# A listed order of 2,500 steps found anew: attention followed by a gated feed-forward block on one core

## The chip, the core and the metric

The kernel runs on one core of a Trainium2 chip. A core has a matrix engine (TensorE, "PE" in the profile; its weight loads are shown as "PEld"), VectorE ("DVE"), ScalarE ("ACT"), GpSimd ("POOL") and SyncE ("SP"), which here only issues DMA transfers. Every engine takes its own instructions strictly in the order in which the program lists them, and waits at an instruction until the semaphores that it names have come. The metric is the device time of one execution in microseconds (us). Before the change the median of three runs is 685.67 us (685.07 to 685.78).

## The reference

Two blocks follow each other, all in float32. The first is an attention between 512 tokens and 32 states in each of 8 batches and 8 heads, in both directions. The second takes the 8 x 544 = 4,352 rows that come out of it (544 rows a batch, 512 wide) through a feed-forward layer of width 2,048 with an unusual gate.

```python
def _attn_ref(x, state):            # x (8, 8, 512, 64), state (8, 8, 32, 64)
    scores = scale * np.matmul(x, state.transpose(0, 1, 3, 2))
    a = softmax(scores)             # over the states
    xread = np.matmul(a, state)
    scores2 = scale * np.matmul(state, x.transpose(0, 1, 3, 2))
    a2 = softmax(scores2)           # over the tokens
    sread = np.matmul(a2, x)
    return np.concatenate([xread, sread], axis=2)

def _moe_ref(x, w_in, w_out):       # x (4352, 512)
    h = x @ w_in                    # 512 -> 2048
    sp = np.maximum(h, 0.0) + np.log1p(np.exp(-np.abs(h)))
    g = h * erf(sp)
    return g @ w_out                # 2048 -> 512
```

## The kernel before, in words

**Work and stages.** The token rows of a batch are one unit, A1 to A7 and B0 to B7: the hidden layer is cut in two halves of 1,024, and the A units do the first half for all batches, the B units the second. (Batch 0's first half is done apart, in the head, by the steps h0 to h7 and o00 to o36; the state rows have units of their own, SA and SB.) Each A unit of batch b comes with the attention of batch b; the attention's weights y are kept in DRAM and come back for the B units. The state matrix is multiplied with w_in once a batch (the steps ending in m, called "mixed"), so that xread is never written out: h is y times that product. The large products are cut in the way of Strassen and Winograd: seven products of half blocks instead of eight, with sums and differences before and after. In the first product of a unit these are the steps f01 to f17, in the second one (done twice over, quarter blocks) ap10 to bp71. So TensorE does fewer products, and VectorE many additions: 582 of its 763 instructions are tensor_tensor.

**Steps and the list.** Every piece of work is a named step, registered with `step(name, f)` and issued in the order of one string, `ORDER`, with 2,532 names. The string was written by a planner that is not part of the kernel. The last lines of the kernel read it and tie each engine's instructions to that order. A name `~k*n` is no step: it issues n filler products on bank k, whose results nobody reads.

```python
    for name in ORDER.split() or do:
        if name[0] == "~":
            k, n = name[1:].split("*")
            issue(name, lambda: warm(bank[int(k)][:, 0:P], int(n)))
        else:
            issue(name, do.pop(name) if ORDER.split() else do[name])
    in_order(begun)
```

The list interleaves all engines, so it tells two things: the order on each engine, which binds, and where the planner thought a step on one engine would start beside those on the others, which does not. In the trace of the kernel before, the steps of VectorE and ScalarE start within 3.6 us of the TensorE step listed next, mostly 0.4 to 1.1 us ahead of it.

**Names that the change and the prediction touch** (lines are those of the profile):

- Loads. lx0 to lx3 (L341): batch 0's x in four pieces of 256 KB, lx0 and lx2 on ScalarE's queue, lx1 and lx3 on SyncE's. lst0 (L346): batch 0's state, 64 KB; ls1 (L369): batch 1's; lst1 to lst8 (L365): the rest, on GpSimd's queue. i0l0 to i3l1 and o0l0 to o3l1 (L394): halves of w_in and w_out, 512 KB each. a1xq0 to a1xq7 (L354): batch 1's x, in small pieces, two transfers a step, all on SyncE's queue.
- Conversion of each half weight: a0 and a1 on ScalarE (L379, L381), v0 on VectorE (L383), v1 on VectorE or, for i2, i3 and o0 to o3, on GpSimd (L385).
- Batch 0's attention. x00 to x31 transpose the pieces (L444), s0 the state (L450), the steps ending in c copy the results out of PSUM. t0 and t1 (L456) are the token scores, 16 products of 64 columns each as the trace counts them, q0 and q1 (L463) the state scores. Each half k of the tokens runs through max, less (subtract), exp (ScalarE), sum, inv, norm, ta (transposes, L469) and tac (copy to y).
- First unit. n00, n01, n02, n10, n12 (L961): w_in mixed with the state; h0L to h7R (L972): h products, which need both y (tac) and the mixed pieces; h0s to h7s softplus (L693), h0e and the like erf (L988), each behind a table load of ScalarE when the function changes. big0 to wn1, tw0, tw1, rd0 (L539), rn0, rt0 (L549): batch 0's state attention. a1tx0 to a1tx3 (L250) transpose batch 1's x; a1s (L564) are batch 1's scores.
- Attention of batch b, after the scores: a2sb0 and a2nm0 and the like (L587, L596) subtract the maximum and multiply by the inverse sum; from batch 2 on they run on GpSimd. These twelve and the six conversions are GpSimd's 18 tensor instructions.
- VectorE's additions with two operands in SBUF: t01 to t64 (L243; sums of w_out's blocks, `twice`, L934), y01 and the like, A1a2, A1b3, A2b4+ and the like (`inner_sums`), A1g0 and the like (the gate, L244).
- Stores. res holds seven half blocks of results. A1D0 and the like (L735) add a half block to the output in DRAM, on GpSimd's queue; A1d0 and the like write it first, on SyncE's. The copy that reuses the place in res (A1ac11, A1au2) waits until the store has landed.
- The end: B7p71 is TensorE's last step; B7C120, B7C121, B7v20 to B7v31 are additions, B7d10 to B7d31 the last stores.

Of the kernel before, what the change touches and what calls it, by code (L numbers as in the profile page):

```python
# [52 lines left out]
A1bp71 a3ty0 A1bp51 A1bu3 y31 A3f01 a3kz A3m01 A1b4 A2f1s12 A1D0 A1bp20 A3M1 A3f0c t54 A2f1s22
A1bp21 y32 A1bp40 A3M2 A1b4+ A1bp41 A3M3 A2e0 A3f06 y34 A1bc22 A3f02 A3M4 y33 A1bp30 A3f0c11 A2g0
a3z2 A3f0u2 a3z1 A3f05 A2e1 a3z0 a3z3 A3f07 A1d3 a4tx2 A3f11 A3f0u3 A1bp31 A1bc21 A3f0c22 A3f04
A1bc11 a3iy A1bc12 A2ap10 A3f0c21 A2g1 A1d1 A3f1c A3f03 yl3 A3f16 rd3 A2q A3f1u2 A3f17 A3f0c12
rn31 rn30 A2A1 rt3 A2ap50 A3f1u3 rc3 A1D1 A2A3 A3f14 A2ap11 A3f0s11 A2A2 A2ap51 A2ac A2a2 A3f12
A2A4 A3f15 a4s A1U2 A2a3 A1D4 A2ap60 a4c0 A3f0s21 a5xq6 A2b2 A2ap61 a4c1 A3f1c22 A2ap20 A2au2
# [6 lines left out]
A4f0u2 A2bp30 A2D0 A2bc11 A4M4 A4f0c11 A4f07 a5tx2 A2bp31 A4f0u3 A4f11 A2bc12 a4z1 a4iy a4z2 A4f04
A4f0c22 a4z3 A3g1 a4z0 A4f03 A4f0c21 A2d3 A2d1 A3ap10 A4f1c yl4 A4f16 A4f0c12 A4f12 A4f0s12 A2U2
A4f1u2 A3q A4f15 A4f0s11 A4f0s22 A4f17 A2U3 A4f0s21 A3A1 rd4 A4f1u3 A2D1 a5tx0 A4f14 rn40 rn41
A2D2 A3ap11 A3A3 rt4 A3ap50 rc4 A3a2 A4f1c11 A3ac a5s A4f1c22 A3ap60 A3a3 a5c0 a6xq1 a5c1 A3ap61
A3A2 A4f1c21 a6xq7 A2D3 A3ap20 A3au2 a6xq3 a5tu0 A4f13 a6xq2 A3A4 A3ap21 A3ap70 A3ac11 a5mx0
A4f1s11 A3ap71 A4f1s12 a6xq0 A4f1c12 a5sb0 A3ap51 A4f1s22 a5my0 A3au3 a6xq5 A3bp10 A4f1s21 A3ac22  # L70
A3bp11 A3ap40 A3a4 A2D4 a5ex0 A3ap41 A3b2 a5x2 A3ap30 A3ac21 a6xq4 a5sm0 A3bc A3ap31 a5ey0 a5iz
A3bp60 A3b4+ a5ey1 A3ac12 a5nm0 A3bp61 a6tx0 A3bp20 A3bp21 A4e0 a5x1 A3bp50 A3b3 a5x3 A3d2 A5m
a5ta0 A3d3 A3bu2 A3b4 A3bp51 a5ty0 A5m00 A3bp70 a5ty1 A5m10 A5m11 y51 A3bp71 a5kz A5f01 A5M1 a6xq6
A3bu3 A5m01 y52 A3bp40 A5M2 A5f0c A4e1 A3bc22 A3bp41 a5iy A5f06 y53 A5M3 A5f02 A5M4 A5f0u2 A5f05
A4g0 A5f0c11 A5f07 a5z0 A3bp30 a5z3 A5f0u3 A3d0 y54 A3bc11 A5f0c22 A3bp31 a5z2 a5z1 A5f04 A3bc12
a5x0 A4g1 A5f11 A5f0c21 A4ap10 A5f1c A3bc21 A5f03 A3d1 A4q A5f16 yl5 A3D0 A5f0s12 A5f0c12 A5f12
# [6 lines left out]
A6m01 A4bp50 A6M1 a6ty0 A6f01 A4b3 a6kz A5e0 A4bp51 a7xq0 A6f05 y62 A6M2 A4D0 a7xq4 A4bp70 a6iy
A6M3 A6f0c A4bp71 A6M4 A4bc11 a7xq5 A6f06 A4b4+ A4bu3 y63 A6f02 a7xq7 A4b4 A6f0u2 y64 A4bp40 A5g0
A6f0c11 A6f07 a6z0 a6x2 A6f11 a6z2 A6f0u3 a6x3 A4bc22 A5e1 A4bp41 a6z3 A6f0c22 A6f04 a6z1 a7tx0
yk5 A4bp30 A4bc21 A5g1 A6f0c21 A6f03 A6f1c A4bp31 A6f16 A6f0c12 A6f12 A6f0s22 A4bc12 A6f1u2 A5ap10
A5q A4d1 yl6 A6f17 a7tx2 rd6 A6f1u3 A6f1c11 A5A1 A6f15 rn61 a7x2 rn60 A4U2 rt6 A5ap50 rc6 A6f1c22
# [1 line left out]
A4U3 A6f0s11 a7tu0 A6f1s22 A5ap61 A4D4 A5ap51 A5a3 A5au2 i5+l A4D3 A6f1s12 A5ap21 a7x3 A6f1s11
a7mx0 A5ap70 A6f0s12 A5ac11 A6f1c12 a7sb0 A5ap71 a7my0 A6f1s21 A5bp10 A5au3 A5ac22 A5bp11 A5ap40  # L90
A5a4 A4D2 a7x0 a7ex0 A5ap41 A5b2 a7ey0 A5ap30 a7ey1 A5b4+ A5ap31 a7sm0 A5ac21 A7m A5bc a7iz A5ac12
a7nm0 A5d0 A6e0 a7x1 A5bp60 A5d2 A5bp20 a7ta0 A7m01 A5bp50 A7m00 A5bp21 A7m10 a7ty0 A5d3 A5bp51
A7m11 y71 A5bp61 A5b3 A7f01 A5bu2 y73 A5bp70 A7M1 yk7 y72 A5bp71 A7M2 A7f05 A5D0 A5bu3 A7M3 A7f0c
A5bp40 A5b4 A6e1 a7ty1 A7f06 A5bc22 a7kz A5bp41 A7M4 A7f0u2 A7f02 y74 A6g0 A7f07 A7f0c11 A5bp30
# [1085 lines left out]
```

## Time and profile before

| what | value |
|---|---|
| median of three runs | 685.67 us (685.07 to 685.78) |
| the profiled execution's own time | 685.86 us |
| its span, first to last instruction | 684.0 us |
| TensorE products | 5,586, busy 675.3 us |
| VectorE, ScalarE, GpSimd busy | 583.7, 488.4, 126.2 us |
| granted TensorE clock, mean | 0.999 |
| first product, end of the last product | 0.78 us, 679.07 us |
| ScalarE table loads | 63 (1.28 us each) |
| filler products in the list | 8 at the start, then 2 + 3 + 1 + 3 + 1 |

The span leaves out what the device does before the first and after the last instruction of the program; the time of a run holds it. A group's row on the page has the line, the engine, the operation, what it writes and reads, its busy time and the mean of one, and the idle time before it. A timeline row has the start, the length and the same names; "x5" merges five instructions that follow each other. In a row of the windows stand, for each engine, its busy time and in brackets the number of instructions that started in it, then the granted TensorE clock, the share of the DMA engines and the GB/s. A name ending in q means that an engine's sequencer only issued something.

### The profile page before, as it was taken

What the parts mean: (1) busy time and instruction counts of PE and PEld (TensorE: products, weight loads), DVE (VectorE), ACT (ScalarE), POOL (GpSimd) and SP (SyncE); (2) the same over time, 40 slices, a digit from 0 to 9 for tenths busy, and PEclk for the clock granted to TensorE, in tenths of its full rate; (3) what the DMA queues carried; (4) which work ended last, traced back from release to release, by engine and by line L of the source; (5) the groups of instructions that cost most, each with busy time, mean ns of one, the idle gap of its engine ahead of it and who ended that gap; (6) DMA issues with size and microseconds to landing.
All of it is one profiled execution on the core that took longest, in us unless ns stands there. A gap on an engine that the chain in (4) does not pass through costs nothing.

```text
span 684.0 us, 13840 instructions
## 1 busy us (share of the span) xinstructions
PE 675.3 (99%) x5586; PEld 591.3 (86%) x5586; DVE 583.7 (85%) x763; ACT 488.4 (71%) x759; POOL 126.2 (18%) x103
## 2 busy tenths in 40 slices
...
GB/s 301 201 253 125 194 143 172 180 106 186 173 162 132 178 210 176 185 116 140 199 218 222 108 103 84 2 67 20 47 101 62 55 36 82 20 66 16 78 55 124
DMA packets 145839, 87.15 MB, mean 127 GB/s; under 512 B 92784, under 2 KB 138096, under 8 KB 145776
## 3 DMA queue, kind: packets, MB, share of 16 engines
...
q10 hardware_dynamic: 544, 0.52, 0.2%
...
## 4 chain that ended last, share of the span: by engine, by line
PE 87%; DVE 4%; ACT 3%; SPq 3%; DMA 2%; issue 1%; DVEq 0%
PE b L827 44%; PE b L704 24%; PE b L757 5%; PE b L1034 4%; PE b L655 3%; PE b L994 3%; SPq L354 2%; PE b L972 1%; DVE big L250 1%; PE b L539 1%; PE b L564 1%; SPq L359 1%; DMA big<-kept_z 1%; PE b L431 1%; PE b L456 1%
## 5 line engine op out<-in xcount | busy, mean ns | idle before, releaser
L735 POOL DMA_DIRECT2D out_dram<-res x67 | 80.4, 1385 | 433.5 <-DVE res L242 128.0
L827 PE MATMUL b<-big,ring 128*128 128x128 f32 x1196 | 152.7, 276 | 0.0
L827 PEld LDWEIGHTS b<-big,ring 128*128 128x128 f32 x1196 | 145.5, 192 | 6.6 <-issue 2.5
L250 ACT COPY ring<-b 128x512 f32<-128x512 f32 (+1 forms) x136 | 78.4, 584 | 76.2 <-PE b L704 52.6
L704 PE MATMUL b<-y,m 128*128 128x256 f32 x480 | 122.0, 381 | 0.2 <-DVE ring L242 0.2
L250 ACT COPY res<-b 128x512 f32<-128x512 f32 (+2 forms) x125 | 64.2, 522 | 55.8 <-PE b L827 44.0
L704 PEld LDWEIGHTS b<-y,m 128*128 128x128 f32 x480 | 86.7, 191 | 13.0 <-DVE ring L242 1.3
L704 PE MATMUL b<-sy,m 128*128 128x256 f32 x360 | 91.5, 381 | 0.4 <-DVE m L243 0.4
L244 DVE TENSOR_TENSOR ring<-ring 128x2048 f32<-128x2048 f32 (+1 forms) x36 | 77.8, 2168 | 6.9 <-ACT ring L712 5.6
L693 ACT ACTIVATE ring<-ring 128x512 f32<-128x512 f32 x128 | 77.4, 632 | 3.0 <-DVE ring L242 2.5
L827 PE MATMUL b<-ta,ring 128*128 128x128 f32 x548 | 72.3, 276 | 0.0
L704 PEld LDWEIGHTS b<-sy,m 128*128 128x128 f32 x360 | 64.8, 191 | 8.3 <-issue 1.1
L827 PEld LDWEIGHTS b<-ta,ring 128*128 128x128 f32 x548 | 68.5, 192 | 3.8 <-issue 1.7
L827 PEld LDWEIGHTS b<-big,ta 128*128 128x128 f32 x572 | 68.2, 192 | 4.1 <-ACT b L250 1.7
L827 PE MATMUL b<-big,ta 128*128 128x128 f32 x572 | 71.3, 276 | 0.0
L243 DVE TENSOR_TENSOR ring<-ring 128x1024 f32<-128x1024 f32 (+3 forms) x66 | 69.9, 1068 | 0.2
L242 DVE TENSOR_TENSOR ring<-ring,b 128x512 f32<-128x512 f32 (+1 forms) x72 | 47.3, 660 | 23.9 <-ACT ring L250 12.2
L242 DVE TENSOR_TENSOR res<-res,b 128x512 f32<-128x512 f32 (+2 forms) x60 | 36.2, 603 | 33.5 <-PE b L827 18.8
L712 ACT ACTIVATE ring<-ring 128x2048 f32<-128x2048 f32 x30 | 57.3, 1912 | 0.2
L250 ACT COPY b<-b 128x512 f32<-128x512 f32 (+2 forms) x63 | 34.7, 551 | 21.2 <-PE b L827 13.9
L242 DVE TENSOR_TENSOR res<-res 128x512 f32<-128x512 f32 (+1 forms) x56 | 42.1, 753 | 1.1
L242 DVE TENSOR_TENSOR ring<-ring 128x1024 f32<-128x1024 f32 (+1 forms) x35 | 40.0, 1144 | 0.6 <-ACT ring L250 0.3
(150 smaller groups left out, 999.1 us busy)
## 6 DMA issues: line engine op xcount, KB each, us to landing
...
big<-in_x_dram SPq DMA_DIRECT2D x112, 64.0 KB, 2.7
...
```

Of the source, the lines that this page charges most:

```text
L242: add = lambda o, a, b: tt(o, a, b, op=ALU.add)
L243: sub = lambda o, a, b: tt(o, a, b, op=ALU.subtract)
L244: mul = lambda o, a, b: tt(o, a, b, op=ALU.mult)
L250: do[name] = lambda: f(*args)
L655: pe.matmul(out=to[j][e][q, :], lhsT=by, rhs=w_in[r, 4 * j:4 * j + 4, i, :], start=True, stop=True)
L693: act.activation(out=o, in_=i, func=ACTF.Softplus)
L704: pe.matmul(out=to[:, i], lhsT=xs[n - 1][:, q:q + P], rhs=ys[n - 1], start=(start and i == 0), stop=(i == 1), skip_group_check=True)
L712: step(u + "e%d" % o, lambda s=s: act.activation(out=s, in_=s, func=ACTF.Erf))
L735: nc.gpsimd.dma_start(out=to, in_=of, accum_op=ALU.add)
L757: pe.matmul(out=to[:, E2 * h:E2 * h + E2], lhsT=a[:, k // 2, k % 2], rhs=rhs[n][:, k], start=(start and h == 0 and k == 0), stop=(k == 3), ...
L827: pe.matmul(out=out_[:, P * j:P * j + P], lhsT=lhs[:, i], rhs=rhs[:, i], start=(start and j == 0 and i == 0), stop=(i == 1), skip_group_ch ...
L1034: pe.matmul(out=to[:, P * i:P * i + P], lhsT=xs[n - 1][:, i, k], rhs=ys[n - 1][:, k], start=(start and i == 0 and k == 0), stop=(k == 1), ...
```

## The change

Only the string `ORDER` differs. The set of steps is the same, and every step does what it did; the new list has 2,530 names, since there are three filler entries instead of five (2 + 1 + 3 products after the first 8). [...]

In the built program the order differs on every engine from the first steps on; on average a step stands about ten places from where it stood. TensorE has 2,812 product instructions instead of 2,816 (the fillers), ScalarE 60 table loads instead of 63, and the instructions that only wait for a further semaphore change in number: 114 instead of 128 on TensorE, 176 instead of 189 on VectorE, 196 instead of 184 on ScalarE, 124 instead of 109 on SyncE, 98 instead of 97 on GpSimd.

The diff, cut to the head, to the places named above and below, and to the end:

```diff
--- before.py
+++ after.py
@@ -21,161 +21,161 @@
 
 
 ORDER = """
-warm own lx2 lst0 lx3 lx0 lx1 i0l0 i0l1 i1l1 i1l0 x20 s0 x20c s0c0 i2l1 x30 x21 x30c x10 x31 x10c
-x00 s0c1 x31c x11 i2l0 x00c x11c t0 s0c i0a0 i3l1 x21c x01 i0v0 i0a1 max0 x01c i0v1 i0+a0 ~7*2 t1
-i3l0 less0 i0+v0 n00 exp0 max1 q0 n00c0 ls1 i0+a1 sum0 q1 less1 i1a0 inv0 i0+v1 exp1 norm0 o0l1
-~7*3 n01 i1a1 sum1 o0l0 ~7*1 ta0 a1xq0 inv1 q1c n01c1 norm1 n01c0 ta0c n00c1 i1v0 ~7*3 ta1 a1xq3
-i2a0 i1v1 h1L i2a1 h0L i2v0 q0c n02 ta1c i2v1 h0R big0 n02c0 i3a0 big1 ub h1R n02c1 i3a1 ubc a1xq2
-big h3L i3v0 wt0 a1xq5 h0c i3v1 n10 wt1 h1c h3R a1xq7 n10c1 n10c0 h2L o0a1 h3c a1xq6 wz o0a0 ~7*1
-n12 a1xq4 wn1 h5L n12c1 n12c0 a1xq1 y01 tw1 y02 wn0 o1l1 h2R o1l0 h1s y04 o0v0 h0s yl0 tw0 tw1c
-a1tx3 o3l0 o0v1 h3s h5R o3l1 h2c h2s o2l0 a1tx2 h6L tw0c a1tx1 rd0 h5c a1tx0 h0e h7L a1x2 rn0 t01
-a1x3 h2e rt0 h0g h6R rc0 h7R o1a0 h2g a1s o1a1 o1v0 h4L h7c a1c1 o1v1 h6c a1c0 h4R a1tu1 a2xq0 o00
...
-a2xq5 A1f11 a1iy o2v0 A1f0u3 a1x1 A1f0c22 A1f04 o2v1 h4c A1f03 h4s u1c a1z0 A1f0c21 u0c a1z2 o10
-A1f0c12 a1z3 A1f1c a1z1 t11 yl1 T1 A1f16 h6e a2tx2 o3v1 A1f15 h4e o12 a2tx0 A1f1u2 h6g A1f17
...
-A1f1c12 A1f1s11 a3xq1 a2mx0 A1f1s21 a2x2 o14 a2my0 a2sb0 t2k a3xq2 A1e0 t0k o26 a3xq4 t21 A1e1
-A1g0 a3xq6 o06 a2x0 a3xq5 A2m A1g1 yk0 a2ex0 yk1 a2x1 o16 A2m11 a2sm0 a2x3 o0c t3k A2m10 a2ey1 o30
...
-a3ey1 A1ap30 A1ac21 t53 a3iz A1bc A1ap31 t43 A1b3 a3ey0 A1bp60 A2f1c12 a3nm0 A1bp61 A1ac12 A3m
...
-A2ac21 a4sm0 A2ap30 a5xq5 a4ey0 A2ap31 a4ey1 a4iz A2b3 a5xq2 A2bc A4m a4nm0 A2ac12 a5xq4 A3f1s12
-A2bp60 A4m00 A4m01 A2bp50 A2b4+ A4m11 a4ta0 a5xq7 A4m10 A2bp61 A3f1s21 A2bp20 a5xq0 a4ty0 A2bu2
...
-a6ey0 A4ap41 a6sm0 a6ey1 A4ap30 A4ac21 a6iz A4b2 A4ap31 a6nm0 A6m A4ac12 A5f1s21 A4d2 A4bc A5f1s11
...
-A6f0s21 A6f14 A5A2 A4D1 A5ap11 A5a2 yk6 A6f13 A5ac A5A3 A6f1c21 a7s A5A4 A5ap60 a7c0 a7c1 A5ap20
...
-SBpc21 SBd2 B1f16 w13 w14 SBd1 B0ap50 B1f0s22 w23 B1f0c12 B1f1u2 B1f12 w3k SBd3 w42 w4k w03 B0ap11
...
-B7p31 B7pu2 B7w2 B7p70 B7C120 B7w4 B7d10 B7D1 B7C121 B7p71 B7d11 B7v30 B7v20 B7d30 B7v31 B7d20
-B7v21 B7d31 B7d21
+warm lx1 own lx2 lst0 lx3 lx0 i0l0 i0l1 i1l0 i1l1 i2l0 x10 s0 x10c x30 s0c1 s0c0 x11 x30c x20 x00
+x20c x31 i2l1 x00c x21 x11c t0 x31c i0a0 s0c i3l0 i0a1 i0v0 x21c i0v1 i0+a0 x01 i3l1 max0 x01c
+i0+v0 i0+a1 ~7*2 t1 less0 ls1 i0+v1 exp0 o0l0 sum0 i1a0 n00 max1 q0 i1a1 inv0 q1 less1 norm0 exp1
+n01 a1xq7 i1v0 n01c0 ~7*1 ta0 q1c sum1 o0l1 a1xq6 n01c1 ta0c inv1 n00c1 i2a0 norm1 ~7*3 h1L i1v1
+ta1 n00c0 i2a1 i2v0 h0L ta1c q0c i2v1 a1xq3 i3a0 n02 big0 ub h1R big1 i3a1 h0R n02c1 a1xq5 ubc
+n02c0 big i3v0 wt0 n10 a1xq1 h1c h3L i3v1 n10c0 wt1 h0c a1xq4 h2L o0a0 a1tx3 h2R o1l0 a1xq2 n10c1
+o0a1 h3R wz wn0 a1xq0 n12 wn1 h5L o3l1 n12c1 y01 o1l1 h3s tw1 y02 o2l1 n12c0 a1tx2 h0s tw0 h2s
+o0v0 tw1c h5R h2c o0v1 tw0c h3c h1s h6L a1tx1 rd0 a1tx0 h5c h0e h7L a1x1 rn0 y04 h2e o2l0 h0g rt0
+h6R a1x3 rc0 o3l0 o1a0 h7R h2g a1x2 a1s o1a1 o1v0 yl0 h7c h4L a1c1 o1v1 h6c a1c0 h4R a1my1 a1x0
...
+A1m01 A1f06 o3a0 a1ty1 u0 A1M3 a1kz A1f0u2 A1f02 y13 a2xq6 o2a0 A1M4 A1f07 T1 a2xq4 A1f0c11 u1
+A1f0u3 y14 A1f11 a2xq1 o3v0 A1f0c22 A1f04 o3v1 h4s h4c A1f03 A1f0c21 u1c o10 A1f1c A1f0c12 a1z0
+a1z1 y03 a1z3 o2v0 a1z2 A1f16 h4e yk0 a2tx2 o2v1 yl1 A1f12 A1f1u2 t3k a2tx0 h6e A1f15 u0c A1f1c11
...
+a2tu0 o24 A1f1s22 a3xq3 A1f1s12 t12 a2mx0 a3xq1 o06 a3xq6 a2my0 A1e0 a2sb0 a3xq4 o26 A1e1 a3xq5
+A1g0 A2m a3xq2 a2x0 yk1 A1g1 o14 a2ex0 a2x1 A2m00 o0c o16 a2sm0 a2ey1 A2m10 t21 o30 a2ey0 a2iz
...
+A2f13 A1ac11 A1ac22 a4xq6 A1ap40 A1b3 a3x3 A1bp10 a3ex0 A1a4 a3x0 A1bp11 A2f1c11 A1ap41 a3sm0
+a3ey1 A1ap30 a3x2 A1ac21 t52 a3iz A1ap31 A1bc A2f1c12 a3nm0 a3ey0 a4tx0 A1bp20 A1bp21 A1ac12 A3m
...
+A2a4 a5xq4 A1D2 A2ap40 a4ey0 A1D4 A2ap41 A2b4+ A2ac22 A4m a4sm0 a5xq5 A3f0s21 A2b3 A2ac21 A2ap30
+A4m10 a4iz a5tx0 a4nm0 A2bc A2ap31 A4m11 A4m00 A2bp60 A2ac12 A3f1s21 A2bp61 A4M1 A2d3 A2bp20 A2d2
...
+rc4 A4f15 A3ac A3a2 A4f1s11 A2D1 a5s A4f0s21 A4f1c22 A4f0s12 A3ap60 A2U3 a5c1 A3a3 A4f1s22 A3ap61
...
+a6sm0 A4ap40 A4ap41 a6iz a7xq7 A4ac22 a6nm0 A5f1s11 A6m A5f1s22 A4ac21 A4bc A4b3 A4ap30 A6m11
...
+A5ac A4D1 a7s A5a2 a7x2 A5ap20 a7c0 A5A4 a7c1 A6f15 A6f1c11 A5a3 A5ap60 A5ap21 A6f1c22 A4U3
+A6f1s22 A5ap61 a7tu0 A5ac11 A4D4 A5ap50 A6f1c21 A6f0s21 a7mx0 A5bp10 A6f1s11 A5au2 A5bp11 a7my0
...
+B0a2 B1f17 SBpc21 B0A4 B0ac SBd2 B1f15 B1f1u3 w22 B1f1c11 A7D2 B0ap60 w52 B1f1c22 B1f1s11 B0ap20
+w34 B1f1s22 B0a3 B0ap21 B0A3 B1f14 B0ac11 B1f13 w43 yL2 B1f1c21 w24 B0ap51 B0a4 B0ap61 w03 B0b2
...
+B7p60 B6d1 B7p61 B7p31 B7pu2 B7w2 B7p70 B7C121 B7w3 B7d11 B7D1 B7w4 B7p71 B7C120 B7d10 B7v30 B7v20
+B7d30 B7v31 B7d20 B7v21 B7d31 B7d21
```

More of the change, by code (lines that the diff above doesn't have):

```diff
@@ L53 @@
[L53 to L58, printed above, removed]
@@ L65 @@
[L65 to L70, printed above, removed]
@@ L71 @@
[L71 to L76, printed above, removed]
@@ L83 @@
[L83 to L87, printed above, removed]
-A6f0s21 A6f14 A5A2 A4D1 A5ap11 A5a2 yk6 A6f13 A5ac A5A3 A6f1c21 a7s A5A4 A5ap60 a7c0 a7c1 A5ap20
@@ L89 @@
[L89 to L94, printed above, removed]
@@ new lines @@
+A1f0u3 y14 A1f11 a2xq1 o3v0 A1f0c22 A1f04 o3v1 h4s h4c A1f03 A1f0c21 u1c o10 A1f1c A1f0c12 a1z0
+a1z1 y03 a1z3 o2v0 a1z2 A1f16 h4e yk0 a2tx2 o2v1 yl1 A1f12 A1f1u2 t3k a2tx0 h6e A1f15 u0c A1f1c11
+A1f17 a1iy h6g o12 A1f1u3 t61 t01 A1f1c22 rd1 A1f0s22 T2 A1f0s11 A1f14 rn10 a2x3 rn11 A1f0s12 h4g
+rt1 A1f1s11 A1f13 rc1 T4 A1f0s21 a2s A1f1c21 t31 o04 A1f1c12 a2c0 a3xq0 a2c1 t11 t41 A1f1s21 a3xq7
+a2tu0 o24 A1f1s22 a3xq3 A1f1s12 t12 a2mx0 a3xq1 o06 a3xq6 a2my0 A1e0 a2sb0 a3xq4 o26 A1e1 a3xq5
+A1g0 A2m a3xq2 a2x0 yk1 A1g1 o14 a2ex0 a2x1 A2m00 o0c o16 a2sm0 a2ey1 A2m10 t21 o30 a2ey0 a2iz
@@ new lines @@
+A1ap20 a4xq0 A1ap70 t24 a3mx0 a4xq1 A1ap71 a4xq2 A2f1c22 a3sb0 A1ap21 A1au3 a3my0 a4xq5 A2f1c21
+A2f13 A1ac11 A1ac22 a4xq6 A1ap40 A1b3 a3x3 A1bp10 a3ex0 A1a4 a3x0 A1bp11 A2f1c11 A1ap41 a3sm0
+a3ey1 A1ap30 a3x2 A1ac21 t52 a3iz A1ap31 A1bc A2f1c12 a3nm0 a3ey0 a4tx0 A1bp20 A1bp21 A1ac12 A3m
+A2f1s11 t43 t63 A2f1s22 a3ta0 A2f1s21 A2f1s12 A1bp60 t54 A3m00 y31 A1bp61 a3iy A3m10 a3ty1 A3f01
+A3m11 a3ty0 A3m01 A1bp50 t53 A3f0c a3kz t44 A1bu2 y32 A1bp51 y33 A3f02 A3M1 A1bp70 A3M2 A2e0 y34
+A1bp71 A3M4 A3f06 A3M3 A1bu3 A3f05 A1b4 A3f0u2 A3f0c11 A1b4+ A1bp40 A1bc22 A2e1 a3z3 A2g0 A1bp41
@@ new lines @@
+A1d0 A3f07 a3z0 a3z2 A3f11 a3z1 A3f0u3 yk2 A1bc11 a4tx2 A1bp30 A1d3 A1bc21 yl3 A1bp31 A3f0c22
+A3f04 A1d2 A1bc12 A2g1 A3f03 A1d1 A3f0c21 A1D0 A2ap10 A3f1c A3f16 A1U2 rd3 A3f1u2 A2q A3f17 rn31
+rn30 A2A1 A3f12 A3f1u3 A3f0c12 rt3 A3f14 rc3 A2A2 A1D1 A3f15 A1U3 A3f0s11 A2ap11 A2a2 a4s A2ac
+A3f1c22 A2ap60 A2A4 a4c1 a5xq2 a4c0 A2ap20 A3f1c21 a4x3 A2a3 A3f0s12 A2ap21 a4x1 A3f1c11 a4tu0
+a5xq3 A2ap50 A3f1s12 A2ac11 A2ap61 A2A3 A3f1s11 a5xq1 A3f1s22 A3f13 a4mx0 A3f0s22 a5xq7 A2bp10
+A2au2 A3f1c12 a4sb0 a4x0 A2ap70 a4my0 a5xq0 A2ap71 a4ey1 A2bp11 A2b2 A1D3 A2ap51 A2au3 a4x2 a4ex0
@@ new lines @@
+A2bc12 A4f1c11 A4f0c12 A2d1 A4f17 a5tx2 yl4 rd4 A4f1u3 A2U2 A4f14 A3A2 rn41 rn40 rt4 A3ap11 A3A3
+rc4 A4f15 A3ac A3a2 A4f1s11 A2D1 a5s A4f0s21 A4f1c22 A4f0s12 A3ap60 A2U3 a5c1 A3a3 A4f1s22 A3ap61
+A2D3 a5c0 A3ap20 A4f1c21 a5x3 A3A4 a6xq2 A3ap21 a5tu0 A3ap50 A3b2 A3au2 A4f13 A4f1s12 A3ap70 A3b4
+A3ac11 a5mx0 A3ap71 a6xq0 A3ap51 A4f1c12 a5sb0 A3au3 a5x1 a5my0 A4f1s21 A3bp10 a6xq1 A3bp11 A3ac22
+a6xq3 A3ap40 A2D4 A3a4 a5ey1 A3ap41 a5ex0 A3b3 a5x2 A3ap30 A2D2 A3ac21 a5sm0 A3ap31 A3bc a5ey0
+A3b4+ A3bp20 a5iz A3ac12 a5nm0 A3bp21 A3d3 A5m A4e1 a6xq6 a6tx0 a5ta0 A3bp60 A5m11 A5m01 A3bp61
```

217 lines of the change are left out of this document (112 added, 105 removed).

## The prediction

> **What bounds the kernel now.** I read the page's busy totals first, then the windows, then the timeline of the first 40 us, then the places where VectorE and GpSimd overlap, and last the tail. The page:
>
> ```profile
> span 684.0 us, 13840 instructions
> PE 675.3 (99%) x5586; PEld 591.3 (86%) x5586; DVE 583.7 (85%) x763; ACT 488.4 (71%) x759; POOL 126.2 (18%) x103
> ```
>
> TensorE is busy for all but 8.7 us, and the change removes no product: what can move is that rest, stalls that "busy" hides, and filler products. The windows (us; then busy of PE, PEld, DVE, ACT, POOL):
>
> ```profile
> 0.00:10.00 10.00, 8.86 (x51) 7.74 (x52) 2.59 (x7) 4.02 (x7) 1.16 (x7) 1.00 0.83 266
> 10.00:20.00 10.00, 9.16 (x150) 8.03 (x150) 8.77 (x19) 7.91 (x13) 0.00 (x0) 1.00 1.09 340
> ...
> 40.00:60.00 20.00, 19.60 (x94) 11.02 (x93) 19.69 (x37) 19.11 (x29) 10.34 (x12) 1.00 0.92 185
> 60.00:100.00 40.00, 39.82 (x256) 24.12 (x258) 39.27 (x53) 30.73 (x47) 4.29 (x3) 1.00 0.56 145
> 100.00:140.00 40.00, 39.55 (x421) 34.12 (x414) 39.19 (x56) 28.47 (x49) 6.34 (x4) 1.00 0.68 170
> ```
>
> The reader is to see two things. The head (0 to 35 us) is the only stretch with much idle TensorE. And from 40 to 140 us VectorE is busy for 98.2 of 100 us (19.69 + 39.27 + 39.19): time won in the head lasts only if VectorE gets ahead too. From the timelines:
>
> ```profile
> 8.54 1.97 PE L456 MATMUL b<-ring,big 128*128 128x64 f32 x16 [0.36 <-DVE big L250]
> ...
> 19.01 1.25 PE L972 MATMUL b<-y,m 128*128 128x256 f32 x5
> ...
> 33.23 1.10 PE L539 MATMUL b<-big,ring 128*32 128x64 f32 x64 [0.51 <-ACT ring L250]
> ```
>
> ```profile
> 58.39 2.36 DVE L243 TENSOR_TENSOR big<-ta 128x256 f32<-128x256 f32 x1
> ...
> 116.48 1.91 POOL L596 TENSOR_TENSOR big<-big,z 128x1024 f32<-128x1024 f32 x1 [4.71 <-ACT b L250]
> 116.53 2.68 DVE L243 TENSOR_TENSOR big<-ring 128x768 f32<-128x768 f32 x1
> ...
> 123.38 0.38 PE L827 MATMUL b<-ta,big 128*128 128x128 f32 x1 [0.45 <-DVE ta L243]
> ```
>
> The first block holds t0, the first h product (h1L) and rd0. In the second, VectorE's subtraction t11 takes 2.36 us where its like take 0.42, because GpSimd's o3v1 (58.08 to 60.46) runs beside it; A1b3 takes 2.68 for 0.95 beside a3nm0. With t21 (1.23 for 0.42) and A2b4+ (1.54 for 0.42) VectorE loses 1.94 + 1.72 + 0.81 + 1.12 = 5.6 us so, 4.5 of it before 140 us.
>
> **The head, step by step.** Below, each step starts at the latest of its engine's previous start plus that row's start-to-start time and its inputs' ends; all durations are from the timeline. In the trace the pieces of x landed at 4.08 (lx2), 3.59 (lst0), 5.35 (lx3), 5.60 (lx0) and 6.34 (lx1), each w_in half 1.5 us apart from 7.84 on: a full DMA queue.
>
> *x to t0.* New: lx1 and lx2 share the queue first, so about 4.6 each; lst0 5.0; lx0 6.1; lx3 6.3, the total being what it was. TensorE does x10, s0 (1.06 long), then stands until 6.35 for x30, with x11, x20, x00 behind it (0.22 each). VectorE's x20c and x00c (0.34 apart) end at 8.2; t0 at 8.35 instead of 8.54.
>
> *Softmax.* Before, VectorE has i0v1 (0.60) between max0 and less0, max1 (which waits for t1's end at 13.2) ahead of sum0, and i0+v1 (0.55) ahead of norm0. The new list has only i0+v0 (0.34) in the first place, sum0 ahead of max1, and i0+v1 beside exp0: max0 10.35, less0 11.3, exp0 12.05, sum0 12.75, max1 13.35, inv0 13.95, less1 14.3, norm0 14.95, where the trace has 15.95.
>
> *First h products.* h1L stood behind ta1 (norm1 18.47), at 19.01. New: ta0 15.65, ta0c 16.3 to 16.9, and h1L ahead of ta1: 17.1. norm1 ends at 18.2, behind the moved i1v0 (0.60), so ta1 18.3, h0L 18.7 to 19.6.
>
> *n02 to n12.* i1v1 follows norm1: 18.15, was 19.39. So n02 at 19.6, was 20.84; ub, h1R, h0R until 22.3. n10 now waits for GpSimd's i2v1: i2v0 ends at 20.0, 0.14 until GpSimd starts (the trace's lag), 2.41 long, so n10 22.6; all h pieces stand behind it. Before it was 24.80, with h3L (0.96) ahead: 2.2 - 0.96 = 1.2 ahead. Then 0.59 and four h pieces of 0.87: n12 26.65, was 27.53 with one piece (h2R) fewer and a filler (0.31) more: 1.75 ahead.
>
> *To a1s.* ScalarE works without a gap (1.06 a conversion, table load 1.28): h3s 27.7, n12c0 until 28.65, tw0 28.65, was 30.40. h5R, h6L, then rd0 at 30.85 (tw0c ends 30.5, so the 0.51 wait goes), was 33.23: 2.4 ahead. Late next: rn0 stands on VectorE behind a1tx1, a1tx0, h5c until 32.9, so rt0 loses up to 0.4: a1s near 35.1, was 37.16.
>
> So 2.0 ahead by this sum. Ends: 1.0, if only norm0's gain reaches TensorE, and 2.4, rd0's. I take 1.8, since DMA landings shared by two queues are the least certain rows. Fillers fall from ten products to six (4 x 0.22 = 0.9): they stood in waits, so they are in this sum.
>
> Cover that could go: ls1 lands after all of w_in (19.75 in the trace; ub needs it at 20.2); o0l1 goes out behind o0l0 and a1xq7 (before ahead of both), at about 15.7; o0l0 took 6.9 us in that place, so 22.6, and o0a0 needs it at 24.2; every instruction of ScalarE up to h3s and n12c0 is queued behind o0a0. a1xq0 is the last of its kind instead of the first, out near 26.5, landed by 30, needed at 31.7. On GpSimd the eight state loads come in another order: u0's closest one is listed 4.4 us of TensorE work ahead, before it was 3.5 with 0.56 to spare. 0 for these.
>
> **Does it last, part by part.** *VectorE's load.* Summing durations of what is listed ahead of the same product: A1f01 0.4 us less than before, A3f16 the same. With 3.4 us fewer blocks up to there (next item), VectorE can be 1.8 ahead. 0.
>
> [...] Walking each of GpSimd's 18 tensor steps against VectorE's neighbours in the new list: y03 waits 0.25, A1g0 0.85 (one 1.21 reduction runs beside a2sb0's 1.91), A2b2 0.3, A4M1 0.5 (a4nm0 of 1.91 to 2.42 beside 1.75 of other work), A4b3 1.5 (0.14 + 1.91 of a6nm0, with only A4ac22, 0.60, beside it), two of 0.2: 3.8 us, 1.1 of it before 140 us against 4.5. A1b3 moves to beside a3sb0, behind 2.4 us of other work. Its late end made A3m 2.55 where its like take 1.88, and the wait at 123.38 (A1bp71 0.62 late): -1.3. A4b3's block costs 0 (as A2b4+'s 1.12 did at 158 us, with no TensorE wait behind it) to 1.3 (A1b3's); VectorE there is busy for 17.95 of 20 us (220 to 240), nearer the first: +0.3.
>
> [...]
>
> *Result buffers.* GpSimd's accumulating stores land 3.0 to 8.7 us after issue. Three are now listed closer ahead of the copy that reuses their buffer than any before (5.6): SBd2 to B0ac11 4.4, A4D1 to A5ac11 5.45, A2D1 to A3au2 5.5. Each costs 0 (landing 4.5, a copy with 0.5 in hand) to 2.8 or, SBd2, 3.9 (landing 8.7, less lead and 0.5). Most land near 4.5 when nothing is queued in front: +0.2 in all.
>
> *Table loads* 63 to 60: 3.8 us of ScalarE, which is 71% busy and gets none back before 60 us: 0. *Extra semaphore waits on TensorE* 128 to 114: rows behind one such wait start within 0.01 us of the others, only the eight behind two or more are 0.09 late: 0. *Tail:* C120 moves behind C121 and w3; TensorE's last product still ends 5.0 us before the span does, and the moved adds (0.42 to 0.69) have 3.8 us to spare: 0.
>
> **Sum.** -1.8 - 1.3 + 0.3 + 0.2 = -2.6. Against the profiled execution: span 684.0 - 2.6 = 681.4; with the 1.86 outside the span (685.86 - 684.0) 683.3; that execution stands 0.19 over the median, so 683.1.
>
> **Rivals.**
> 1. *The head's gain is given back.* VectorE and ScalarE (19.11 of 20 us at 40 to 60) are nearly full, and any new idle there is lost for good. Then only half the stalls' 1.3 remains: 685.0. For it: 98%. Against: fewer blocks.
> 2. *The clock.* The trace runs at 0.213 us a product until 6.86 us and 0.11 after. The new wait for lx3 (5.4 to 6.35, s0 aside) could delay that beyond t0: 16 products x 0.11 = 1.8, so 684.9. [...]
> 3. *Slower: result buffers.* Every copy behind a late landing waits, and TensorE with it, 1 to 1. With landings of 7.5 us and more at those three places (rows: 7.49, 8.25, 8.75) the waits are 2.6 + 1.55 + 1.5 = 5.6 and up: 682.9 + 5.6 = 688.5. It decides from 4.1 us together (687.0). For it: closer by 1 us. Against: the median landing is 5.2.
> 4. *No change:* planned waits merely move; 685.7.
>
> **How the numbers follow.** 0.2% is 1.4 us, about what a measurement can tell from no change. Forecast 0.68 (faster); rivals 1 0.13, 2 0.06, 4 0.04 (same); 3 0.09 (slower). The range goes from 681.7 (head 2.4, block and stores 0, and two small waits of before, 0.25 ahead of a2s and 0.23 at A6f17, half gone) to 685.8, which takes in rivals 1, 2 and 4: outside remain rival 3 and some 0.06 below.
>
> **What would show it.** Right: t0 near 8.35, h1L near 17, rd0 near 31, a1s near 35; t11 back at 0.42, A1b3 near 1; no wait of 0.6 near 118 to 124 us; last product near 676.5. Wrong: o0a0 waiting for a DMA; TensorE at 0.21 a product past 8 us; the lead at a1s gone by 140 us; copies into res waiting for stores.

## The result and the profile after

The changed kernel takes 683.25 us in the median of seven runs (682.93 to 683.84), the kernel before 685.67 (685.07 to 686.44, seven runs): a ratio of 0.9966, with a 95% interval of 0.9954 to 0.9977. It is 0.34% faster. The profiled execution took 683.49 us with a span of 681.7, against 685.86 and 684.0 before. From the page of the changed kernel:

```profile
span 681.7 us, 13822 instructions
PE 673.8 (99%) x5578; PEld 589.7 (87%) x5578; DVE 579.2 (85%) x763; ACT 483.3 (71%) x756; POOL 125.2 (18%) x103
```

VectorE does the same 763 instructions in 4.5 us less (583.7 before). 3.9 us of this is time by which its steps were longer beside GpSimd's tensor steps than alone: 5.6 us before, 1.7 now (1.46 at A4b3, 0.28 at A4b2). The windows of the changed kernel (us; then busy of PE, PEld, DVE, ACT, POOL, the granted clock, DMA share, GB/s):

```profile
0.00:10.00 10.00, 8.90 (x54) 7.53 (x55) 2.51 (x7) 3.45 (x6) 1.16 (x7) 1.00 0.84 265
10.00:20.00 10.00, 9.25 (x153) 7.62 (x155) 9.68 (x21) 9.14 (x17) 0.00 (x0) 1.00 1.12 344
...
40.00:60.00 20.00, 19.72 (x97) 11.41 (x96) 19.02 (x34) 19.44 (x30) 8.69 (x12) 1.00 0.89 208
60.00:100.00 40.00, 40.00 (x261) 24.31 (x262) 37.64 (x57) 29.46 (x48) 4.93 (x3) 1.00 0.55 143
100.00:140.00 40.00, 40.00 (x425) 35.32 (x414) 39.15 (x58) 29.59 (x50) 6.29 (x4) 1.00 0.67 165
```

From 60 to 140 us TensorE has no gap left (39.82 + 39.55 of 80 before). From 40 to 140 us VectorE is busy for 95.8 us, where it was busy for 98.2. From the timeline of the head:

```profile
8.24 2.00 PE L456 MATMUL b<-ring,big 128*128 128x64 f32 x16
...
17.48 1.10 PE L972 MATMUL b<-y,m 128*128 128x256 f32 x4
...
31.34 1.10 PE L539 MATMUL b<-big,ring 128*32 128x64 f32 x64
...
32.20 1.35 DVE L250 STREAM_TRANSPOSE big<-big 128x512 f32<-128x512 f32 x2 [0.71 <-DMA big<-in_x_dram]
...
34.05 0.28 DVE L250 COPY sn<-b 128x128 f32<-128x128 f32 x1
...
34.38 0.33 PE L549 MATMUL b<-ident,sn 128*128 128x128 f32 x1 [0.88 <-DVE sn L250]
```

These are t0, h1L, rd0, a1tx1 with a1tx0, rn0 and rt0. rd0 is 1.9 us earlier than before (33.23), but rt0 only 0.85 (35.23): TensorE stands 0.88 us there for rn0, and rn0 stands on VectorE behind a1tx1, which waits for a late piece of batch 1's x. The chain of work that ended last (start, length, what) names the two places at which the head is still held up, both DMAs:

```profile
2.26 6.67 DMA big<-in_moe_w_in_dram
27.73 4.34 DMA big<-in_x_dram
```

They are i0l0, the first half of w_in, which lands at 8.93, and a1xq2, the piece that a1tx1 waits for. And from the timelines where GpSimd meets VectorE (A1b3; a3nm0 and A3m; then a6nm0 and A4b3):

```profile
111.01 0.95 DVE L243 TENSOR_TENSOR big<-ring 128x768 f32<-128x768 f32 x1
...
115.63 1.91 POOL L596 TENSOR_TENSOR big<-big,z 128x1024 f32<-128x1024 f32 x1 [4.82 <-ACT b L250]
...
117.39 1.95 PE L655 MATMUL b<-w_in,st 64*32 64x512 f32 x32
```

```profile
229.67 1.91 POOL L596 TENSOR_TENSOR big<-big,z 128x1024 f32<-128x1024 f32 x1 [3.92 <-DVE z L427]
229.99 2.41 DVE L243 TENSOR_TENSOR big<-ring 128x768 f32<-128x768 f32 x1
230.36 1.95 PE L655 MATMUL b<-w_in,st 64*32 64x512 f32 x32
```

A1b3 takes 0.95 us instead of 2.68 and A3m, with no wait inside, 1.95 instead of 2.6 (118.33 to 120.94 in the trace before). The one large block left is A4b3, as foreseen (2.41 for 0.95), and TensorE goes on beside it without a wait.

To see where TensorE got ahead, I put the steps of both lists on one scale: the product time done so far, each kind of step counted at its usual duration in the trace before, fillers at nothing. The lead at a point of that scale is how much earlier a trace reaches it than the trace before. For the changed kernel it is 0.79 us at a1s, 0.93 at 100 us, 2.32 at 130 us and 2.27 at the last product (674.87 against 677.14). So the gain has two parts: under a microsecond from the head, and 1.4 us between 105 and 125 us.

### The profile page after: what moved, and what is told of

Read it like the earlier page. It is cut to its first block, busy times and chain, and to the rows that moved or that the text cites. A ratio compares the mean times of both kernels' runs of the same rounds, so it can differ in the third digit from the quotient of the medians.

```text
span 681.7 us, 13822 instructions
## 1 busy us (share of the span) xinstructions
PE 673.8 (99%) x5578; PEld 589.7 (87%) x5578; DVE 579.2 (85%) x763; ACT 483.3 (71%) x756; POOL 125.2 (18%) x103
## 4 chain that ended last, share of the span: by engine, by line
PE 93%; DVE 2%; ACT 2%; DMA 2%; issue 0%; SPq 0%; DVEq 0%; ACTq 0%
PE b L827 47%; PE b L704 26%; PE b L757 5%; PE b L994 4%; PE b L655 4%; PE b L1034 4%; PE b L564 1%; PE b L539 1%; DMA big<-in_moe_w_in_dram 1%; DMA big<-in_x_dram 1%; PE b L972 1%; ACT ta L379 0%; DVE w_in L385 0%; ACT big L381 0%; DVE ring L250 0%
## 5 line engine op out<-in xcount | busy, mean ns | idle before, releaser
L827 PE MATMUL b<-big,ring 128*128 128x128 f32 x1196 | 150.8, 275 | 0.0
L250 ACT COPY ring<-b 128x512 f32<-128x512 f32 (+1 forms) x136 | 78.3, 585 | 94.1 <-PE b L704 68.0
L704 PE MATMUL b<-y,m 128*128 128x256 f32 x480 | 120.6, 381 | 0.0
L250 ACT COPY res<-b 128x512 f32<-128x512 f32 (+2 forms) x125 | 64.8, 524 | 47.3 <-PE b L827 36.0
L243 DVE TENSOR_TENSOR ring<-ring 128x1024 f32<-128x1024 f32 (+3 forms) x66 | 69.3, 1054 | 0.1
L250 ACT COPY b<-b 128x512 f32<-128x512 f32 (+2 forms) x63 | 34.6, 549 | 20.8 <-PE b L704 9.1
```

The source lines that it names most:

```text
L243: sub = lambda o, a, b: tt(o, a, b, op=ALU.subtract)
L250: do[name] = lambda: f(*args)
L704: pe.matmul(out=to[:, i], lhsT=xs[n - 1][:, q:q + P], rhs=ys[n - 1], start=(start and i == 0), stop=(i == 1), skip_group_check=True)
L827: pe.matmul(out=out_[:, P * j:P * j + P], lhsT=lhs[:, i], rhs=rhs[:, i], start=(start and j == 0 and i == 0), stop=(i == 1), skip_group_ch ...
```

## The experiments

All of them change only the string ORDER. Their listings are three lines shorter, so L240 there is L243 above, L247 is L250, L969 is L972, and so on. The kernel before, run beside them, had medians of 685.58 to 685.63.

### The two parts, each alone

The first experiment has the order of the changed kernel up to a1s and the rest in the order of before; the second has the order of before up to a1s and the rest in the changed order. The first lines of the first one's diff:

```diff
-warm own lx2 lst0 lx3 lx0 lx1 i0l0 i0l1 i1l1 i1l0 x20 s0 x20c s0c0 i2l1 x30 x21 x30c x10 x31 x10c
...
+warm lx1 own lx2 lst0 lx3 lx0 i0l0 i0l1 i1l0 i1l1 i2l0 x10 s0 x10c x30 s0c1 s0c0 x11 x30c x20 x00
...
```

> The changed list up to a1s, the rest in the order of the kernel before. In the two traces TensorE is 0.93 us ahead at 100 us and 2.3 us ahead from 125 us on. Theory (two gains that add: 0.9 from the head, kept, and 1.4 from the stalls at A3m and A1bp71, which this list still has): 685.67 - 0.9 = 684.8 us, A1b3 near 2.7 us beside a3nm0. Rival (VectorE is full from 40 to 140 us, so that a gain of the head alone is given back): 685.5 us or more.

> The kernel before up to a1s, the rest in the order of the changed list. Theory (two gains that add): only the 1.4 us at 117 to 124 us remains, 684.3 us, A1b3 near 0.95 us, no wait of 0.6 us there. Rival (the new rest pays only with the new head's VectorE ahead): 685.3 us or more.

The new head alone: 685.22 us (684.09 to 686.85), ratio 0.9985 (0.997 to 1.0). The lead is 0.85 us at 50, at 100 and at 200 us: what the head wins is not given back while VectorE is at its fullest. At 254 us 0.3 of it goes at rd6, which waits for data that come back from DRAM (first row). The stalls near 118 us are there as before (second and third row; A3m 2.62):

```profile
254.44 1.10 PE L536 MATMUL b<-big 128*32 128x64 f32 x64 [0.50 <-DMA big<-kept_z]
```

```profile
115.68 2.68 DVE L240 TENSOR_TENSOR big<-ring 128x768 f32<-128x768 f32 x1
...
117.47 2.62 PE L652 MATMUL b<-w_in,st 64*32 64x512 f32 x32
```

The new rest alone came out at 685.53 us, ratio 0.9986 (0.9972 to 1.0), against the 684.3 expected. But its eleven times fall in two groups, five from 684.42 to 684.63 and six from 685.53 to 685.95, and its trace, of an execution of the second group (685.66), shows why: the lead grows from 0.4 to 1.79 between 100 and 125 us as the theory has it, and falls to about 0.6 by 200 us:

```profile
158.49 1.25 DVE L247 STREAM_TRANSPOSE big<-big 128x1024 f32<-128x1024 f32 x1 [3.56 <-DMA big<-in_x_dram]
...
160.36 1.60 PE L824 MATMUL b<-big,ring 128*128 128x128 f32 x12 [0.36 <-DVE res L239]
```

a5tx0 waits 3.56 us for a5xq0, which SyncE issued at 150.69, behind a4x0's 256 KB, and which landed at 158.31. (In the changed kernel the same wait is 1.14 us and TensorE doesn't feel it.) So one more run, the seventh experiment, with this edit to the second one's list:

```diff
-a5xq3 A2ap50 A3f1s12 A2ac11 A2ap61 A2A3 A3f1s11 a5xq1
+a5xq3 a5xq0 A2ap50 A3f1s12 A2ac11 A2ap61 A2A3 A3f1s11 a5xq1
...
-a4my0 a5xq0 A2ap71
+a4my0 A2ap71
```

> The second experiment's list (old head, new rest) with a5xq0 moved in SyncE's queue ahead of a5xq1, a5xq7 and a4x0. In that experiment's trace VectorE waits 3.56 us at a5tx0 for a5xq0, which lands at 158.31, and TensorE loses 0.9 us at A2bp50 and A4f01 behind it; its times fall in two groups, near 684.5 and near 685.7. Theory (this landing is what took the gain): no wait at a5tx0, one group, 684.4 us. Rival (the rest of the changed list needs the new head's VectorE): 685.3 us or more.

684.30 us, all eleven from 684.08 to 684.48; ratio 0.9981 (0.9972 to 0.9990). The wait at a5tx0 is gone and with it the second group. The new rest is worth 1.33 us without the new head.

### The block at A1b3, taken out and put back

The third experiment, in the kernel before:

```diff
-t53 a3iz A1bc A1ap31 t43 A1b3 a3ey0
+t53 t43 A1b3 a3iz A1bc A1ap31 a3ey0
```

> The kernel before with two VectorE steps, t43 and A1b3, moved ahead of a3iz, so that GpSimd's a3nm0 starts behind them instead of beside A1b3. Theory (A1b3's block by GpSimd is what makes A3m and A1bp71 late): A1b3 0.95 us instead of 2.68, A2f1c12 ends near 118.1 instead of 119.8, both waits go, 685.67 - 1.3 = 684.4 us. Rival (the waits come from where A2f1c12 and t63 stand in the list, not from the block; or the time won is lost in VectorE's next waits): 685.4 us or more.

684.27 us (683.78 to 685.27); ratio 0.9974 (0.9961 to 0.9987): 1.36 us for two steps of VectorE that change places with one. A1b3 (first row) is over before GpSimd's a3nm0 starts, and A3m takes its 1.95 us:

```profile
115.72 0.95 DVE L240 TENSOR_TENSOR big<-ring 128x768 f32<-128x768 f32 x1
...
117.30 1.92 POOL L593 TENSOR_TENSOR big<-big,z 128x1024 f32<-128x1024 f32 x1 [5.91 <-DVE z L424]
...
117.94 1.95 PE L652 MATMUL b<-w_in,st 64*32 64x512 f32 x32
```

The sixth, the opposite edit in the changed kernel:

```diff
-A1ap40 A1b3 a3x3
+A1ap40 a3x3
...
-a3iz A1ap31 A1bc
+a3iz t43 A1b3 A1ap31 A1bc
...
-A2f1s11 t43 t63
+A2f1s11 t63
```

> The changed kernel with t43 and A1b3 put back behind a3iz, as the list before has them, so that A1b3 runs beside GpSimd's a3nm0 again. Theory (the block by GpSimd is what the change takes away there): A1b3 near 2.7 us instead of 0.94, A2f1c12 ends near 118.5 and A3m gets its wait of 0.7 us back, with a further wait behind it up to 1.3 in all: 683.9 to 684.7 us. Rival (the new order has room enough on VectorE there, as at A4b3, which takes 2.41 us with no TensorE wait behind it): 683.3 us.

685.89 us (685.26 to 687.15), ratio to before 1.0002 (0.9993 to 1.0011): the whole gain of the change is gone, and more than expected.

```profile
116.11 1.92 POOL L593 TENSOR_TENSOR big<-big,z 128x1024 f32<-128x1024 f32 x1 [4.82 <-ACT b L247]
116.16 2.68 DVE L240 TENSOR_TENSOR big<-ring 128x768 f32<-128x768 f32 x1
...
117.87 2.70 PE L652 MATMUL b<-w_in,st 64*32 64x512 f32 x32
...
119.49 0.18 PEld L652 LDWEIGHTS b<-w_in,st 64*32 64x32 f32 x14 [0.62 <-DVE ring L239]
```

a3nm0 starts 0.05 us ahead of A1b3, and A1b3 takes 2.68 us. TensorE loses 0.76 us in A3m, 0.85 behind A1bp61 and 0.19 behind A1bp71, 1.80 together: here VectorE's lost 1.73 us reach TensorE one to one, where they cost the list before 1.3. (At 50 us this execution was already 0.35 us behind that of the eighth experiment, by what the next section shows.)

### The head: where 1.8 us became less than 1

The fourth experiment, in the changed kernel:

```diff
-h6L a1tx1 rd0 a1tx0 h5c h0e h7L a1x1 rn0 y04
+h6L rd0 rn0 a1tx1 a1tx0 h5c h0e h7L a1x1 y04
```

> The changed kernel with rn0 moved on VectorE ahead of a1tx1, a1tx0 and h5c. In its trace a1tx1 waits for batch 1's x until 32.20, rn0 ends at 34.33 though rd0 ends at 32.45, and TensorE stands 1.04 us at rt0. Theory (this place is where the head's gain fell from 1.9 at rd0 to 0.8 at a1s, and TensorE's lead lasts): rn0 ends near 32.8, rt0 right behind h7L, a1s near 35.4 instead of 36.4, 682.3 us. Rival (VectorE, which wins nothing by this, holds TensorE back later, as it is busy for 98% from 100 to 140 us): a1s early all the same, but 683.0 us or more.

The head came out as the theory has it, rn0 at 32.82, rt0 at 33.55, a1s at 35.48, which is 1.68 us ahead of the trace before (37.16), where the changed kernel is 0.79 ahead. And the time did not: 684.32 us (684.02 to 688.99), ratio 0.9983 (0.9965 to 1.0001), slower than the changed kernel. At A1f01 the lead is down to 0.32 us (48.70 against 49.02 before; 48.16 in the changed kernel). The rows of rn0, a1ta0 and A1f01:

```profile
32.82 0.29 DVE L247 COPY sn<-b 128x128 f32<-128x128 f32 x1 [0.28 <-PE b L536]
...
47.85 1.30 DVE L247 STREAM_TRANSPOSE y<-big 128x512 f32<-128x512 f32 x2
48.70 1.10 PE L701 MATMUL b<-y,m 128*128 128x256 f32 x4 [0.90 <-ACT big L601]
```

The first of the two transposes in the second row is a1ta0, which ends at 48.55 (47.94 in the changed kernel, where A1f01 starts at 48.16); A1f01 needs it and starts 0.15 us behind it. (The row names ScalarE, whose part, A1m00, was done at 47.91.) VectorE has no break over 0.15 us from 33.4 to 55 us, and it came into this stretch late: 0.74 us of wait at a1tx2, where a1xq4 landed at 29.97 instead of 28.39, and 0.28 for rd0 at rn0's new place. The rival won: here VectorE sets the pace, and TensorE's lead alone buys nothing. Why the edit came out slower than the changed kernel is less clear. a1xq4 is no step that it moves (28.4 to 29.5 in the other traces with this head), and of the 0.61 us by which a1ta0 is later the wait for rd0 explains 0.28 at most. The rest may belong to this one execution, but all eleven are slower than the changed kernel's median, so the cause stays open. The experiments from here on try to give VectorE time, beside a second measurement of the changed kernel, the eighth experiment.

> The changed kernel once more, beside the next three. Expected 683.3 us; its trace also tells how far the first landings move between executions of one program (lx3 6.47, i0l0 8.93, t0 8.24 in the first trace).

683.67 us (682.97 to 684.77), ratio 0.9971 (0.9959 to 0.9984). Its landings are those of the first trace within 0.2 us (lx3 6.61, i0l0 9.01, t0 8.38). The thirteen runs of the changed kernel together have a median of 683.49.

The fifth, in the changed kernel:

```diff
-a1xq4 h2L o0a0 a1tx3 h2R o1l0 a1xq2 n10c1 o0a1 h3R wz wn0 a1xq0
+a1xq4 a1xq2 a1xq0 h2L o0a0 a1tx3 h2R o1l0 n10c1 o0a1 h3R wz wn0
```

> The changed kernel with a1xq2 and a1xq0 ahead of o1l0 in SyncE's queue. VectorE waits 0.71 us at a1tx1 for a1xq2, which lands at 32.08 behind o1l0's 512 KB. Theory (VectorE, not TensorE, is what sets the pace after the head, so time given back to VectorE there lasts): a1tx1 at 31.5 or before, rn0 0.6 earlier, a1ta0 (47.94, which A1f01 needs at 48.16) 0.6 earlier, 682.7 us. Rival (the time is lost in the next waits of VectorE on ScalarE, 0.70 us at h4c and 0.97 us at A1g0): 683.2 us.

684.41 us (682.99 to 686.24), ratio 0.9974 (0.9957 to 0.9992): no gain. The wait at a1tx1 is gone, but the profiled execution says little on that, since it had lost a microsecond ahead of it. The rows are the transposes of x from x30 on, and t0:

```profile
6.57 2.82 PE L441 MATMUL b<-ident,big 128*128 128x128 f32 x12 [0.24 <-DMA big<-in_x_dram]
9.18 2.48 PE L453 MATMUL b<-ring,big 128*128 128x64 f32 x16
```

The twelve products start 0.213 us apart and take 2.82 us, where the same twelve took 1.83 in the first trace of the changed kernel. They come closer (0.112 us) only from 10.38 us on, in t0. In the sixth experiment's trace this is at 10.38 as well, with t0 at 9.60. That is the second rival of the prediction. The ninth experiment closes the gap in which it may arise, with three fillers behind s0 in the changed kernel:

```diff
-x10 s0 x10c x30
+x10 s0 ~7*3 x10c x30
```

> The changed kernel with three filler products behind s0. In the traces with its head the rate of the first products rises from 0.21 to 0.11 us a product before s0 ends (6.3 us) in four executions; in two (the fifth and sixth experiments) it is still low there, TensorE then stands until lx3 lands (6.5 to 6.95), and the low rate goes on to 9.9 us, 3.4 us and more after that gap: t0 1.0 to 1.4 us late. Theory (the gap before x30 is what puts the rise off): with the gap filled no execution is late by this, t0 at 8.3 to 8.6, the spread of the times narrower than 682.93 to 684.77 (13 runs of the changed kernel), median 683.2 us. Rival (the rise comes at a time of its own, whatever TensorE does): late executions remain, t0 past 9.1 in some, 683.6 us.

683.26 us (682.72 to 684.06, twelve runs), ratio 0.9960 (0.9947 to 0.9974). None of the four profiled executions with fillers has the late rise. In this one the rate is still low in s0 (0.98 us long; 0.65 in the third experiment) and high from the second filler product on, at 6.46:

```profile
6.25 0.94 PE L428 MATMUL b<-ident 128*128 128x128 f32 x6
7.02 1.77 PE L441 MATMUL b<-ident,big 128*128 128x128 f32 x12
```

But the gap alone can't be what delays the rise. In the first trace of the changed kernel, one of the four in which I took the rate to rise before s0 ends, it is low to the end of s0 as well (first row, 1.12 us), TensorE stands 0.26 us ahead of x30, and x30's products come at the high rate at once (second row):

```profile
5.14 1.12 PE L450 MATMUL b<-ident,ring 128*64 128x128 f32 x8
...
6.52 1.83 PE L444 MATMUL b<-ident,big 128*128 128x128 f32 x12 [0.26 <-DMA big<-in_x_dram]
```

And at two late executions in six, four without one come by chance one time in five ((2/3)^4 = 0.2). So neither the cause of the late rise nor the fillers' help is shown. The highest time is lower (684.06 against 684.77), the median within the changed kernel's own two (683.25 and 683.67): a gain that can't be told from none.

The tenth experiment has the ninth's list with the fifth's order of a1xq2, a1xq0 and o1l0; the eleventh has this besides:

```diff
-o3l1 n12c1
+o3l1 h3c n12c1
...
-tw0c h3c h1s
+tw0c h1s
```

> The same with a1xq2 and a1xq0 ahead of o1l0, as in the fifth experiment, whose execution started t0 0.8 us late and was level with the changed kernel again at 48 us (a1ta0 47.32 to 47.37). Theory (that landing costs VectorE 0.5 to 0.7 us, hidden there by the late start): a1tx1 without a wait, a1ta0 0.5 to 0.8 us earlier than 47.3, 682.7 us. Rival (given back at VectorE's waits on ScalarE at h4c and A1g0): 683.2 us.

> The same with VectorE's copy h3c moved ahead of n12c1, into the 0.64 to 0.84 us that VectorE waits there for n12. Theory (VectorE's work sets the pace from 30 to 50 us, so each 0.67 us that it need not do later counts): rn0 right behind rd0, no wait at rt0, a1ta0 another 0.4 to 0.7 us earlier, 682.3 us. Rival (TensorE or ScalarE bounds by then): as without the move, 682.7 to 683.2 us.

683.90 us (683.28 to 684.83), ratio 0.9970 (0.9957 to 0.9983), and 683.97 (683.02 to 685.85), ratio 0.9969 (0.9955 to 0.9984): neither theory. Both profiled executions are at the slow end of these, 684.83 and 685.85, and show a cover that was used up. From the tenth experiment's trace, o1a0 on ScalarE and o1v0 on VectorE:

```profile
37.13 1.13 ACT L376 ACTIVATE ta<-big 128x1024 f32<-128x1024 f32 x1 [1.38 <-DMA big<-in_moe_w_out_dram]
...
38.29 0.69 DVE L380 TENSOR_SCALAR ta<-ta 128x1024 uint32<-128x1024 uint32 x1 [1.37 <-ACT ta L376]
```

o1a0 waits for o1l1, which landed at 37.04 (38.07 in the eleventh, 35.45 in the changed kernel). Moving o1l0 behind the small pieces put the halves of w_out closer to their use, and when a1xq6 landed 1 us late in these two executions (25.6 and 25.4 against 24.67), VectorE lost 1.37 and 2.75 us at o1v0. The order alone doesn't make o1l1 late: in the fifth experiment's trace, with the same order of DMAs, a1xq6 landed at 24.83 and o1l1 at 35.49. What the two edits are worth without that is left open. The twelfth and last leaves the DMAs alone and starts from the ninth experiment's list:

```diff
-o3l1 n12c1
+o3l1 h3c n12c1
...
-tw0c h3c h1s h6L a1tx1 rd0 a1tx0 h5c h0e
+tw0c h1s h6L h5c y04 a1tx1 rd0 a1tx0 h0e
...
-rn0 y04 h2e
+rn0 h2e
...
-o1v0 yl0 h7c
+h7c o1v0 yl0
```

> The changed kernel with the three filler products of the ninth experiment and the order of the DMAs left as it is; four copies and sums of VectorE are moved into its waits: h3c ahead of n12c1 (0.81 us idle there), h5c and y04 ahead of a1tx1 (0.25 to 0.71 us idle), h7c ahead of o1v0. Theory (VectorE sets the pace from 30 to 50 us): rn0 near 33.3 instead of 33.6 to 34.1, rt0 right behind h7L, a1ta0 0.5 to 0.7 us earlier than 47.0 to 47.4, 682.7 us. Rival (ScalarE, with o1a0 waiting for o1l1 until 35.4 and busy for 19.4 of 20 us from 40 on, holds VectorE to the old times): 683.3 us.

683.86 us (683.39 to 684.33), ratio 0.9971 (0.9958 to 0.9983): no gain, and the trace shows a loss of my own making:

```profile
30.42 2.41 POOL L382 TENSOR_TENSOR ta<-ta,big 128x1024 uint32<-128x1024 uint32 x1 [4.70 <-DVE ta L380]
...
31.41 1.71 DVE L240 TENSOR_TENSOR sy<-y,sy 128x256 f32<-128x256 f32 x1
...
34.56 0.33 PE L546 MATMUL b<-ident,sn 128*128 128x128 f32 x1 [1.22 <-DVE sn L247]
```

y04 takes two operands from SBUF, and I had put it beside GpSimd's o0v1: 1.71 us instead of 0.41, rn0 at 34.26 instead of 33.3, and 1.22 us of wait at rt0. How much of the missing gain this accounts for was not tried. No version that I ran beats the changed kernel by more than the runs can tell.

## Why the prediction was right, and where its terms were not

The forecast (683.1 us), the side and the likeliest case hold. Its sum of -2.6 us stands against -2.27 at the last product and -2.4 between the medians. Term by term:

- **Head, -1.8.** Mis-sized, and the largest term that failed. In the two traces it is 0.93 at 100 us. Some 0.4 of that belongs to the one execution of before, in which the product rate rose at 6.9 us; in the three other traces with the old head it rose between 4.5 and 5.5, and they are 0.38 to 0.41 us ahead of it already at t0. The new head alone measures 0.41 by its median, with an interval that reaches from 0 to 2.1 us. So the list's head is worth about 0.4 to 0.5 us by these traces and that median, where I gave it 1.0 to 2.4. t0 came as walked (8.24, forecast 8.35); two later statements failed. max0, forecast at 10.35, starts at 10.84, since i0v1 ahead of it needs i0a1, which needs i0l0: I kept w_in's landings as they were, and i0l0 landed at 8.93 instead of 7.84 (part of this is wander: 7.84 to 8.95 in the four traces with the old order). From there all steps run 0.3 to 0.5 late, down to rd0 (31.34, forecast 30.85). And a1xq0, "out near 26.5, landed by 30" and priced at nothing, went out at 28.27 and landed at 32.54, with a1xq2 at 32.08: rn0, held by a1tx1, a1tx0 and h5c "until 32.9" in the walk, starts at 34.05. At rt0 this cost 1.0 us of TensorE's lead. And the fourth experiment shows that the lead would not have lasted anyway: A1f01 waits for VectorE.
- **Stalls at A3m and A1bp71, -1.3.** Right in mechanism and size: -1.36 by the third experiment, -1.33 for the whole new rest in the seventh, 1.4 us of lead in the changed kernel's trace.
- **A4b3's block, +0.3.** The block is there as worked out (2.41 us; 1.5 forecast, 1.46 measured) and costs nothing. The other blocks in my list did not come, but for A4b2's 0.28: y03 takes 0.42, A4M1 0.68, A1g0 the 2.29 that it took before. VectorE lost 1.7 us in all where I had 3.8. That walk had each two-operand step of VectorE wait for a GpSimd step that had started first, which was my estimate; t11 in the trace before agrees with it (started 0.31 us behind o3v1, ended 0.29 behind it). The rows shown of such meetings came out so: a6nm0, a3nm0 in the sixth experiment and o0v1 in the twelfth had started first (by 0.32, 0.05 and 0.99 us), and VectorE's step ended 0.82, 0.81 and 0.29 us behind them.
- **Result buffers, +0.2.** Nothing: the stores landed at 418.55 (SBd2; B0ac11 starts at 419.32), 259.31 (A4D1; A5ac11 at 260.62) and 181.42 (A2D1; A3au2 at 182.35). The third rival falls with them, though by 0.8 to 1.3 us only.
- **Terms at nothing.** The tail holds: TensorE's last product ends 4.9 us before the span does, as before (679.03 of 684.0). o0a0 did not wait for its data, and no row speaks against the table loads and the extra waits at nothing.
- **Rivals 1 and 2.** "The head's gain is given back" is wrong for what the head really won (0.85 in the first experiment's trace, kept to 200 us) and right for anything more than VectorE wins (fourth experiment). The late rise of the rate came in two of the six profiled executions with this head and no fillers. No run shows that a wait of TensorE is what delays it. I had it as a case for the median; it is a matter of single executions, and costs 0.35 us or less by 50 us, not the 1.8 I gave it.

So the sum was nearer than its largest term, and that is in part luck: the head was over-sized by 0.9 us in the traces, and the two terms of +0.5 for blocks and buffers, which did not come, took up half of that. The parts, -0.41 and -1.33, make -1.7 where the whole change shows -2.0 and -2.4 in its two measurements. The intervals of the two parts (0 to 2.1 us and 0.7 to 1.9 us) take in the difference. The wait at rd6 in the first experiment's trace, which the changed kernel doesn't have, cost that execution 0.33 us of lead; whether it is a cause was not tried.
